# Strassen block products in the second matmul of an FFN: seven products of halves for seven of nine token blocks

## The chip, the cores and the metric

One Trainium2 chip, one core of it. The metric is the device time of one execution in microseconds (us), and the kernel before was timed in three runs: 1028.28, 1029.17 and 1034.58 us, median 1029.17 us. TensorE (PE) multiplies, with its weight loads (PEld) beside it; VectorE (DVE), ScalarE (ACT) and GpSimd (POOL) do the elementwise work; SyncE (SP) issues most of the transfers.

## What is computed

Attention over 4 batches of 576 tokens and 8 heads (block-causal, blocks of 64), then two layers with a feed-forward network (FFN) each. The change concerns the second one:

```
X = fft(fft(x, axis=1), axis=2)
u = x + real(X)
un = (u - mean(u)) / sqrt(var(u) + 1e-6)
ch = relu(un @ w_ch1) @ w_ch2          # 512 -> 2048 -> 512
out = u + ch
```

All of it is in float32 precision. The kernel reaches that with float16 matmuls: every operand is kept as a part `hi` (float16 of the value) and a part `lo` (float16 of what is left), and a product is three matmuls: hi*hi, hi*lo and lo*hi, summed in PSUM.

## The kernel before

The 2304 tokens stand in nine blocks of 256: E0 to E3 and F0 to F3 (first and folded second part of each batch) and L (what is left of all four). `X[c]` holds a block's tokens as two tiles of 128 rows, 512 float32 features wide.

For a block the second FFN runs in three steps. **LN** (`ln`, `ln_hi`, `ln_lo`, L442 to L501) norms the two tiles, splits them on ACT (L491) and DVE (L497) and has SP transpose them by DMA (L498) into `xnT`, of which there is one buffer: a block's transposes can start only when the first product of the block before has read it. **g1** (`gemm1`, L513) makes the 2048 hidden features in eight slots: a slot is 24 matmuls of 256 columns (L530) into one of five PSUM banks, and `g1_out` empties it with two instructions, ReLU into `hi` on ACT (L539) and `max(x,0) - hi` into `lo` on DVE (L540). **g2** (`gemm2`, L547; `gemm2_both` for E0, L577) multiplies by `w_ch2`: for each of the two token tiles 16 x 3 matmuls of 512 columns (L555, L585) into one bank, and `g2_out` (L564) adds the scaled result to `X` into an extra tile on DVE (L570) and SP writes it out (L575).

The second FFN's blocks go E0, F0, E1, F1, E2, F2, E3, F3, L. `ffn_items` writes them as g1 of a block, then its g2, with the LN steps of the next block between the last four parts of the g2. The DFT (`dft_*`) runs beside the first of these blocks and ends in `dft_b_left` (pool tile `u`, L1203 to L1216) while F0's g1 runs. Its constants and the first half of `w_ch1` (two tiles) live in one SBUF pool, `dpool`, which stays open to the end. Another pool has nine slots of 8 KB per partition, tag `w`; from here on they hold the second half of `w_ch1` (two) and all of `w_ch2` (four, until F0's g2 is over). `w_ch2` comes as int64 bits in float64, is decoded once, spilled to DRAM as float32, read back (L373) and split with its scales (L300, L308).

The order of the work is made twice. `merge` (L1022) takes the streams' items by a virtual clock (each item has a cost and things it needs) and calls them; then the framework sorts each engine's instructions by priority (`tc.high_priority(n)` moves them forward) into one fixed order per engine, in which each instruction waits for semaphores. Every engine works strictly in its order.

Of the kernel before, what the change touches and what calls it, by code (L numbers as in the profile page):

```python
# [82 lines left out]

@with_exitstack
def fused_kernel(ctx: ExitStack, tc: tile.TileContext, io: dict):
# [203 lines left out]
    def w_hi(ffn, which, c):  # L289
# [90 lines left out]
    def w_items():  # L380

# [181 lines left out]

    def g2_out(ffn, c, t, ps):  # L564
        x = X[c]
        if ffn == 1:
            dst = x[:, t, :]
        else:
            dst = D_["p"].tile([128, 2, DM], F32, tag=("xe", "xo")[t], name="out")[:, 0]
        nc.vector.scalar_tensor_tensor(  # L570
            out=dst, in0=ps, scalar=W["inv", ffn][:, 0:1], in1=x[:, t, :],
            op0=ALU.mult, op1=ALU.add,
        )
        if ffn == 2:
            nc.sync.dma_start(out=io["out"][slot_of[c] + t], in_=dst)  # L575
# [17 lines left out]
    def ffn_slots(ffn, c):
        s = []
        for mp in range(MT // 2):
            s.append((2.62, lambda mp=mp: gemm1(ffn, c, mp)))
        for t in range(2):
            for part in range(4):
                s.append((2.59, lambda t=t, part=part: gemm2(ffn, c, t, part)))
        return s  # L600
# [649 lines left out]
    if True:  # L1250
# [40 lines left out]
        def ffn_items(ffn, order, both=(), mixed=None):  # L1291
            seq = []
            for n, c in enumerate(order):
                x = ("X", ffn, c) if ffn == 2 else ("X1", c)
# [182 lines left out]
```

## Time and profile before

| | us |
|---|---|
| three runs | 1028.28, 1029.17 (median), 1034.58 |
| span of the profiled execution, first to last instruction | 1034.0 |
| PE busy | 941.8 (91%) |
| DVE busy | 618.7 (60%) |
| ACT busy | 501.4 (48%) |

The profiled execution's own time is not given apart from its span; among the three runs only the slowest, 1034.58 us, is as long as the span, so that is taken for it: span 1034.0 us and 0.6 us around it. In the page's slices a digit is the busy share of 1/40 of the span (25.85 us) in tenths, and in its row PEclk the clock that TensorE was granted. A matmul's duration in a group of lines includes its way through the array; the time from one to the next is read from the chain of waits, whose row gives the total of so many.

### The profile page before, as it was taken

What the parts mean: (1) busy time and instruction counts of PE and PEld (TensorE: products, weight loads), DVE (VectorE), ACT (ScalarE), POOL (GpSimd) and SP (SyncE); (2) the same over time, 40 slices, a digit from 0 to 9 for tenths busy, and PEclk for the clock granted to TensorE, in tenths of its full rate; (3) what the DMA queues carried; (4) which work ended last, traced back from release to release, by engine and by line L of the source; (5) the groups of instructions that cost most, each with busy time, mean ns of one, the idle gap of its engine ahead of it and who ended that gap; (6) DMA issues with size and microseconds to landing.
All of it is one profiled execution on the core that took longest, in us unless ns stands there. A gap on an engine that the chain in (4) does not pass through costs nothing.

```text
span 1034.0 us, 18330 instructions
## 1 busy us (share of the span) xinstructions
PE 941.8 (91%) x7226; PEld 642.5 (62%) x7226; DVE 618.7 (60%) x1501; ACT 501.4 (48%) x884; POOL 83.6 (8%) x217
## 2 busy tenths in 40 slices
PE   5476869898989989999998979999999999999998
PEld 3464744475575575676584746767668577586673
DVE  4799888686867876774396979864332332222120
ACT  5698965676767677534366665632111021120110
POOL 2100101001102002040011111100000000000000
PEclk8588989899999999999998989999999999999999
DMA  7995834666658668456315375620010100201100
GB/s 215 234 253 154 257 72 113 130 130 139 148 96 173 125 128 151 73 138 176 72 60 128 87 226 202 217 77 18 25 31 11 41 21 22 31 22 31 31 11 21
DMA packets 172439, 110.84 MB, mean 107 GB/s; under 512 B 146893, under 2 KB 155094, under 8 KB 170816
## 3 DMA queue, kind: packets, MB, share of 16 engines
q1 hardware_dynamic: 170032, 105.41, 41.3%
q0 software_dynamic: 2320, 4.25, 1.8%
q8 instruction: 57, 0.93, 0.4%
q14 instruction: 30, 0.25, 0.1%
HBM read 59.95 MB, written 11.01 MB: 69 GB/s over the span
## 4 chain that ended last, share of the span: by engine, by line
PE 44%; DVE 6%; DMA 5%; ACT 2%; issue 1%; POOL 0%; ACTq 0%; DVEq 0%; POOLq 0%
PE g L530 19%; PE g L555 19%; DMA wr<-in_w 4%; PE g L585 3%; DVE ws L215 1%; ACT wr L233 1%; DMA xnT1L<-xs 1%; DVE hT L540 1%; PE pq L1189 1%; ACT sign L208 1%; PE ya L1158 1%; DVE ws L212 1%; DVE wq L308 1%; PE pq L1179 1%; PE pf L1179 1%
## 5 line engine op out<-in xcount | busy, mean ns | idle before, releaser
L530 PEld LDWEIGHTS <-wq 128*128 128x128 f16 x3456 | 337.7, 99 | 69.0 <-ACT wq L300 8.2
L555 PE MATMUL g<-wq,hT 128*128 128x512 f16 x1440 | 334.8, 382 | 0.0
L555 PEld LDWEIGHTS <-hT 128*128 128x128 f16 x1440 | 140.7, 98 | 164.8 <-issue 9.6
L539 ACT ACTIVATE hT<-g 128x512 f16<-128x512 f32 x144 | 84.7, 591 | 244.0 <-PE g L530 243.9
L540 DVE SCALAR_TENSOR_TENSOR hT<-g,hT 128x512 f16<-128x512 f32 x144 | 98.6, 687 | 138.6 <-ACT hT L539 138.2
L679 PE MATMUL pv<-vh,PT 128*128 128x65 f16 (+1 forms) x800 | 105.2, 203 | 33.5 <-DMA PT<-P 30.5
L679 PEld LDWEIGHTS <-PT 128*128 128x128 f16 x1200 | 83.6, 100 | 57.7 <-DMA PT<-P 33.1
L891 PE MATMUL st<-k,qz 128*128 128x512 f16 (+2 forms) x288 | 81.5, 338 | 15.8 <-ACT e L913 15.8
L913 ACT ACTIVATE e<-st,aq,acf 128x384 f32<-128x384 f32 (+2 forms) x80 | 56.8, 741 | 60.9 <-DVE aq L908 54.8
L704 DVE SCALAR_TENSOR_TENSOR P<-e,P 128x768 f16<-128x768 f32 (+2 forms) x64 | 62.0, 971 | 38.2 <-ACT P L703 38.0
L585 PE MATMUL g<-wq,hT 128*128 128x512 f16 x288 | 66.6, 389 | 0.3 <-DVE wq L308 0.3
L679 PE MATMUL pv<-vl,PT 128*128 128x64 f16 (+1 forms) x400 | 65.8, 202 | 0.1
L703 ACT ACTIVATE P<-e 128x768 f16<-128x768 f32 (+2 forms) x64 | 54.7, 859 | 5.0 <-DMA PT<-P 3.6
L491 ACT ACTIVATE xs<-xn 128x512 f16<-128x512 f32 x36 | 22.4, 626 | 62.2 <-DMA xnT2('E', 3)_10327<-xs 7.9
L497 DVE TENSOR_TENSOR xs<-xn,xs 128x512 f16<-128x512 f32 x36 | 24.7, 687 | 46.0 <-ACT xs L491 46.0
L195 ACT ACTIVATE ws<-wr 128x512 f32<-128x512 f32 (+1 forms) x48 | 39.3, 829 | 26.2 <-DMA wr<-in_w 23.7
L907 DVE TENSOR_REDUCE aq<-st 128x2 f32<-128x768 f32 (+2 forms) x48 | 46.6, 973 | 8.7 <-PE st L891 5.1
L212 DVE SCALAR_TENSOR_TENSOR ws<-ws,sign 128x512 int32<-128x512 int32 (+1 forms) x48 | 41.5, 867 | 17.2 <-ACT sign L208 14.0
L208 ACT ACTIVATE sign<-wr 128x512 f16<-128x512 f32 (+1 forms) x48 | 46.7, 974 | 9.3 <-DMA wr<-in_w 4.8
L585 PEld LDWEIGHTS <-hT 128*128 128x128 f16 x288 | 28.7, 100 | 34.6 <-issue 3.1
L731 PE MATMUL st<-raw 128*128 128x128 f32 (+1 forms) x128 | 37.3, 421 | 12.2 <-ACT e L749 7.0
L215 DVE SCALAR_TENSOR_TENSOR ws<-wr,ws 128x512 int32<-128x512 int32 (+1 forms) x48 | 41.3, 862 | 0.4
(387 smaller groups left out, 1296.2 us busy)
## 6 DMA issues: line engine op xcount, KB each, us to landing
wr<-in_w SPq DMA_DIRECT2D x16, 1024.0 KB, 6.3
wr<-in_w SPq DMA_DIRECT2D x32, 512.0 KB, 4.1
rawv<-in_vt SPq DMA_DIRECT2D x16, 320.0 KB, 3.7
rawqk<-in_kt SPq DMA_DIRECT2D x16, 288.0 KB, 2.8
out<-out SPq DMA_DIRECT2D x18, 256.0 KB, 2.0
d<-ws SPq DMA_DIRECT2D x4, 1024.0 KB, 5.1
ws<-d SPq DMA_DIRECT2D x4, 1024.0 KB, 8.0
rawqk<-in_qt SPq DMA_DIRECT2D x32, 80.0 KB, 3.4
```

Source lines behind the costliest of these rows:

```text
L208: nc.scalar.activation(out=z[:, :, :, 1], in_=hw.bitcast(F32), func=AF.Copy, scale=float(2.0 ** -100))
L212: nc.vector.scalar_tensor_tensor(out=di, in0=di, scalar=3, in1=zi, op0=ALU.logical_shift_left, op1=ALU.bitwise_or)
L530: nc.tensor.matmul(out=ps[:, i, :], lhsT=w1(ffn, k, wh, m), rhs=xt[:, xh, k, :], start=(n == 0), stop=(n == 3 * KT - 1),)
L539: nc.scalar.activation(out=h[:, :, 0, :], in_=ps, func=AF.Relu)
L540: nc.vector.scalar_tensor_tensor(out=h[:, :, 1, :], in0=ps, scalar=0.0, in1=h[:, :, 0, :], op0=ALU.max, op1=ALU.subtract,)
L555: nc.tensor.matmul(out=ps, lhsT=h[f // 4][:, f % 4, hh, t * 128:(t + 1) * 128], rhs=w2(ffn, f, wh), start=(f == 0 and hh == 0 and wh == 0) ...
L585: nc.tensor.matmul(out=g2["b"][t], lhsT=h[f // 4][:, f % 4, hh, t * 128:(t + 1) * 128], rhs=w2(ffn, f, wh), start=(f == 0 and hh == 0 and ...
L679: nc.tensor.matmul(out=out[..., 0:w], lhsT=l, rhs=v[..., 0:w], start=(n == 0), stop=(n == len(mm) - 1))
L703: nc.scalar.activation(out=P[:, 0, 0:n], in_=e, func=AF.Copy, scale=PSC)
L704: nc.vector.scalar_tensor_tensor(out=P[:, 1, 0:n], in0=e, scalar=PSC, in1=P[:, 0, 0:n], op0=ALU.mult, op1=ALU.subtract)
L891: nc.tensor.matmul(out=st[:, h, 0:n] if j < 4 else sf[:, o:o + n], lhsT=qz[:, a, q:q + 128], rhs=k[:, c, o:o + n], start=(i == 0), stop=(j ...
L913: nc.scalar.activation(out=e[:, h], in_=st[:, h], func=AF.Exp, scale=cf, bias=nb[:, h:h + 1],)
```

## The change

Seven of the second FFN's blocks (all but E0 and F0) take another way through both products.

Second product (`s_gemm2_steps`): the block's hidden features are halved by feature (0 to 1023, 1024 to 2047) and by token tile, `w_ch2` is halved by feature and by output column, and in place of eight products of halves there are seven, of sums and differences of halves (Strassen's algorithm in Winograd's form). A product is 8 x 3 matmuls of 256 columns into one of three PSUM banks. The first two products (`mm(1)`, `mm(2)`) leave out their last eighth (i = 7) until both have done i = 0 to 6. `got(p)` adds a product, or a running sum `su`, to quarters of `X` in place; `put(t)` writes a tile out.

First product (`s_gemm1`): slot i makes features i and i + 8 (of 16 tiles of 128), so that both halves lie in the same bank, and `s_out` empties it in eight instructions where there were two: two ReLUs on ACT into a float32 tile `r`, four sums and differences of 128 columns on DVE, one copy of 896 columns on ACT (`hi` of seven operands), one subtraction of 896 columns on DVE (`lo`). They go into tiles `hs` of the tag `w`.

Weights (`t_items`): the DFT's pool is closed after `dft_b_left`, and a pool of seven tiles T (56 KB per partition) opens in its place; each T is one of the seven operands made of `w_ch2`'s halves. `w_ch2` is read back from DRAM a second time (`wt`, four loads of 1 MB, for j = 0 and j = 1 two each), and for each j and each T: for four of the seven a subtraction on DVE (1024 columns, chained), a copy on ACT (1024 columns, `hi`) and a multiply and subtract on DVE (1024 columns, `lo`). `t_balance` works out power-of-two scales, some eleven instructions on at most four columns. The `w_ch1` tiles of `dpool` get a pool of their own, and outputs of all blocks of the second FFN are now made in place in `X`.

```
 def w_tile(ffn, which, c):
     if ffn == 2 and which == 1:
-        return wst["pool"].tile([128, 2, 2048], F16, tag="w", bufs=2, name=f"wq{ffn}{which}{c}")
+        return wst["w1"].tile([128, 2, 2048], F16, tag="w", bufs=2, name=f"wq{ffn}{which}{c}")
...
+    def t_items(close, needs):
...
+        def build(j, nm):
+            a, b = src[j, 0], src[j, 1]
...
+            x, y, z = {
+                "B11": (b11, None, None), "B21": (b21, None, None), "B22": (b22, None, None),
+                "T1": (b11, b12, b11), "T3": (b12, b22, b12), "T2": (b11, b22, b11),
+                "T4": (b21, b21, b11),
+            }[nm]
+            if y is not None:
+                nc.vector.tensor_tensor(out=x, in0=y, in1=z, op=ALU.subtract)
+            sc = W["tk"][:, 4 + j:5 + j]
+            f = slice(4 * j, 4 * j + 4)
+            nc.scalar.activation(out=T[nm][:, 0, f], in_=x, func=AF.Copy, scale=sc)
+            nc.vector.scalar_tensor_tensor(
+                out=T[nm][:, 1, f], in0=x, scalar=sc, in1=T[nm][:, 0, f],
+                op0=ALU.mult, op1=ALU.subtract,
+            )
...
 def g2_out(ffn, c, t, ps):
     x = X[c]
-    if ffn == 1:
-        dst = x[:, t, :]
-    else:
-        dst = D_["p"].tile([128, 2, DM], F32, tag=("xe", "xo")[t], name="out")[:, 0]
+    dst = x[:, t, :]
...
+    def s_out(ps, h, j):
+        r = fpool.tile([128, 8, 128], F32, tag="hT", bufs=4, name="hr")
+        rf = r.rearrange("p b t -> p (b t)")
+        for q in range(2):
+            nc.scalar.activation(
+                out=rf[:, 256 * q:256 * q + 256], in_=ps[:, q, :], func=AF.Relu,
+                scale=W["tk"][:, j + 2 * q:j + 2 * q + 1],
+            )
+        for o, a, b, op in (
+            (4, 0, 2, ALU.add), (6, 1, 0, ALU.subtract), (5, 4, 1, ALU.subtract),
+            (7, 3, 5, ALU.subtract),
+        ):
+            nc.vector.tensor_tensor(out=r[:, o], in0=r[:, a], in1=r[:, b], op=op)
+        nc.scalar.activation(out=h[:, 0], in_=r[:, 1:8], func=AF.Copy)
+        nc.vector.tensor_tensor(out=h[:, 1], in0=r[:, 1:8], in1=h[:, 0], op=ALU.subtract)
...
+        def mm(p, hb, nm, i0=0, i1=8):
+            if i0 == 0:
+                st[p] = d_tile("s2")
+            ps = st[p][:, 0:256]
+            for i in range(i0, i1):
+                h = hT[2, c][i // 2][:, i % 2]
+                for hh, wh in ((0, 0), (0, 1), (1, 0)):
+                    nc.tensor.matmul(
+                        out=ps, lhsT=h[:, hh, hb], rhs=T[nm][:, wh, i],
+                        start=(i == 0 and hh == 0 and wh == 0), stop=(i == 7 and hh == 1),
+                    )
...
+        return [
+            (2.3, lambda: mm(1, A11, "B11", 0, 7)),
+            (2.3, lambda: mm(2, A12, "B21", 0, 7)),
+            (0.6, lambda: (
+                mm(1, A11, "B11", 7, 8), got(1), mm(2, A12, "B21", 7, 8), got(2),
+            )),
+            (2.6, lambda: (mm(6, S2, "T2"), got(6))),
+            (2.6, lambda: (mm(5, S1, "T1"), got(5))),
+            (2.6, lambda: (mm(7, S3, "T3"), got(7))),
+            (2.6, lambda: (mm(3, S4, "B22"), got(3), put(1))),
+            (2.6, lambda: (mm(4, A22, "T4"), got(4), put(0))),
+        ]
...
+                if ffn == 2 and c not in PLAIN2:
+                    g1 = [(2.62, lambda i=i, c=c: s_gemm1(c, i), (("W", 2, 1, 3),), None) for i in range(8)]
...
+        WT = t_items(dctx.close, (("X", 2, "L"), ("W", 2, 2, 3)))
...
+            (S_D, R_T, WT),
```

PE's order is unchanged up to the end of F0's g2. Three places after that show what is new. The first is DVE in the g1 of block F1; before, one instruction per slot (`g1` is the bank, `hT` the hidden features):

```order
L540 SCALAR_TENSOR_TENSOR hT_9311<-g1_9312,hT_9311 128x2x256
L540 SCALAR_TENSOR_TENSOR hT_9311<-g1_9339,hT_9311 128x2x256
L540 SCALAR_TENSOR_TENSOR hT_9366<-g1_9367,hT_9366 128x2x256
L540 SCALAR_TENSOR_TENSOR hT_9366<-g1_9394,hT_9366 128x2x256
L540 SCALAR_TENSOR_TENSOR hT_9421<-g1_9422,hT_9421 128x2x256
```

and now (`hr` is the tile r of a slot, `hs` its seven operands):

```order
L701 TENSOR_TENSOR hr_9616<-hr_9616 128x128 x4
L703 TENSOR_TENSOR hs2_9590<-hr_9616,hs2_9590 128x896
L701 TENSOR_TENSOR hr_9650<-hr_9650 128x128 x4
L703 TENSOR_TENSOR hs2_9590<-hr_9650,hs2_9590 128x896
L701 TENSOR_TENSOR hr_9685<-hr_9685 128x128 x4
```

A slot's four sums stand behind the `lo` (L703) of the slot before, and that `lo` behind ACT's copy (L702) of its own slot; ACT's order is two ReLUs and the copy, slot by slot.

The second place is DVE behind the end of the DFT (`u` is its last result) in F0's g1; before, four slots are emptied and the LN of E1 and F1 follows:

```order
L1216 TENSOR_TENSOR XxL_3227<-XxL_3227,u_8704 128x512
L540 SCALAR_TENSOR_TENSOR hT_8709<-g1_8710,hT_8709 128x2x256
L540 SCALAR_TENSOR_TENSOR hT_8709<-g1_8737,hT_8709 128x2x256
L540 SCALAR_TENSOR_TENSOR hT_8764<-g1_8765,hT_8764 128x2x256
L540 SCALAR_TENSOR_TENSOR hT_8764<-g1_8792,hT_8764 128x2x256
```

and now the 22 instructions of the T tiles stand among them; the end of that stretch, the last of which stands ahead of everything of E1's g1 (`wt11` is the last load, `g2_8940` the second half of F0's g2):

```order
L440 TENSOR_TENSOR wt10_8867<-wt11_8869,wt10_8867 128x4x256
L444 SCALAR_TENSOR_TENSOR tB21_8757<-wt11_8869,tk_8135,tB21_8757 128x1024
L444 SCALAR_TENSOR_TENSOR tB22_8758<-wt11_8869,tk_8135,tB22_8758 128x1024
L444 SCALAR_TENSOR_TENSOR tT3_8760<-wt10_8867,tk_8135,tT3_8760 128x1024
L440 TENSOR_TENSOR wt10_8867<-wt11_8869,wt10_8867 128x4x256
L577 TENSOR_TENSOR xs_9457<-xn_9455,xs_9457 128x512
L440 TENSOR_TENSOR wt11_8869<-wt11_8869,wt10_8867 128x4x256
L444 SCALAR_TENSOR_TENSOR tT2_8761<-wt10_8867,tk_8135,tT2_8761 128x1024
L647 SCALAR_TENSOR_TENSOR XxF0_3226<-g2_8940,winv2_8146,XxF0_3226 128x512
L444 SCALAR_TENSOR_TENSOR tT4_8762<-wt11_8869,tk_8135,tT4_8762 128x1024
```

So T's last four tiles for j = 1 wait for the fourth load, and the last one also for F0's result. The third place is SP's queue, where that load stands (`xnT2` are the transposes):

```order
L427 DMA wt00_8763<-d220_7394 128x2048
L427 DMA wt01_8765<-d222_7877 128x2048
L427 DMA wt10_8867<-d221_7657 128x2048
L652 DMA out_0<-XxE0_204 128x512 x2
L578 DMA_TRANSPOSE xnT2('E', 1)_8972<-xs_8987 128x8x128
L427 DMA wt11_8869<-d223_8044 128x2048
L578 DMA_TRANSPOSE xnT2('E', 1)_8972<-xs_9005 128x8x128
```

Three loads find free slots of the tag `w` early. `wt11` takes the slot of `wt00`, so it waits until DVE has used that for the last time (T2 of j = 0), and E1's second transpose is queued behind it.

## Rows read from the trace of the kernel before

**Rows 1.** The page's 40 slices: busy tenths and granted clock.
```profile
PE   5476869898989989999998979999999999999998
DVE  4799888686867876774396979864332332222120
PEclk8588989899999999999998989999999999999999
```
**Rows 2.** Chain of waits, its end: start us, us, engine, what, line, count.
```profile
666.14 20.72 PE g L585 x96
...
738.43 20.96 PE g L530 x192
759.39 20.72 PE g L555 x96
...
1009.47 20.73 PE g L555 x96
1030.23 0.75 DVE out L570
```
**Rows 3.** Timeline of ACT and DVE: two slots of E1's g1, then three dependent DVE instructions.
```profile
741.09 0.60 ACT L539 ACTIVATE hT<-g 128x512 f16<-128x512 f32 x1 [13.94 <-PE g L530]
741.71 0.69 DVE L540 SCALAR_TENSOR_TENSOR hT<-g,hT 128x512 f16<-128x512 f32 x1 [2.50 <-ACT hT L539]
...
704.06 0.47 DVE L1207 SCALAR_TENSOR_TENSOR u<-pq,dinv,qc 128x256 f32<-128x256 f32 x1
704.57 0.69 DVE L1213 TENSOR_TENSOR XxE<-XxE,u 128x512 f32<-128x512 f32 x1
705.18 0.69 DVE L1216 TENSOR_TENSOR XxF<-XxF,u 128x512 f32<-128x512 f32 x1
```
**Rows 4.** Groups by line and shape, whole span: count, busy us, mean ns, idle before.
```profile
L958 DVE TENSOR_TENSOR N<-pv,rr 128x128 f32<-128x128 f32 x32 | 9.2, 287 | 0.4
L497 DVE TENSOR_TENSOR xs<-xn,xs 128x512 f16<-128x512 f32 x36 | 24.7, 687 | 46.0 <-ACT xs L491 46.0
L1118 DVE TENSOR_TENSOR xo<-XxE,XxF 128x1024 f32<-128x1024 f32 x4 | 4.9, 1218 | 0.0
L1075 DVE SCALAR_TENSOR_TENSOR ge<-xe,dsc,ge 128x1024 f16<-128x1024 f32 x4 | 5.1, 1276 | 0.2 <-ACT ge L1074 0.2
L703 ACT ACTIVATE P<-e 128x768 f16<-128x768 f32 x32 | 27.2, 849 | 1.8 <-DMA PT<-P 1.4
L703 ACT ACTIVATE P<-e 128x1024 f16<-128x1024 f32 x16 | 16.9, 1057 | 1.6 <-DMA PT<-P 0.9
L1199 ACT ACTIVATE qc<-pq,dinv 128x255 f32<-128x255 f32 x8 | 3.8, 473 | 8.3 <-PE pq L1189 8.2
```
**Rows 5.** Timeline of DVE: end of the DFT, then the LN statistics of F2.
```profile
709.35 0.69 DVE L1216 TENSOR_TENSOR XxL<-XxL,u 128x512 f32<-128x512 f32 x1
...
728.49 0.18 DVE L449 BATCH_NORM_AGGREGATE ln2('F', 2)_9952<-bn2('F', 2)0_9953 128x2 f32<-128x6 f32 x1
...
732.48 0.16 DVE L466 SCALAR_TENSOR_TENSOR ln2('F', 2)_9952<-ln2('F', 2)_9952 128x2 f32<-128x2 f32 x1
```
**Rows 6.** DMA issues from 660 us on, with KB and us to landing.
```profile
ws<-d SPq DMA_DIRECT2D x2, 1024.0 KB, 7.6
xnT2('E', 1)_8903<-xs SPq DMA_TRANSPOSE x2, 3.6
```
**Rows 7.** Stretches: us, then busy PE, PEld, DVE, ACT, POOL, granted clock, DMA share, GB/s.
```profile
297.40:299.80 2.40, 0.00 (x0) 0.00 (x0) 2.40 (x6) 1.60 (x3) 0.00 (x0) 1.00 0.57 158
299.80:301.80 2.00, 1.93 (x10) 1.43 (x11) 2.00 (x6) 0.00 (x0) 0.00 (x0) 0.54 0.95 225
...
421.10:422.70 1.60, 0.11 (x2) 0.04 (x1) 0.54 (x3) 1.54 (x3) 0.00 (x0) 1.00 0.00 0
423.00:425.00 2.00, 2.00 (x19) 1.29 (x18) 0.70 (x1) 1.84 (x3) 0.00 (x0) 1.00 0.00 0
...
617.00:619.00 2.00, 2.00 (x8) 0.95 (x7) 2.00 (x6) 0.52 (x1) 0.00 (x0) 0.50 0.89 301
```

More of the change, by code (lines that the diff above doesn't have):

```diff
@@ L274, in w_balance, with t_balance @@
         W["inv", ffn] = inv
+    def t_balance():
+        s1, s2 = W["sc", 2, 1], W["sc", 2, 2]
+        z = sm.tile([128, 8], F32, tag="tz", bufs=1, name="tz")
+        eta, m2, r1 = z[:, 0:2], z[:, 2:4], z[:, 4:8]
+        nc.vector.tensor_tensor(out=eta, in0=s1[:, 0:2], in1=s1[:, 2:4], op=ALU.min)
+        nc.vector.tensor_scalar(out=eta, in0=eta, scalar1=0.5, scalar2=None, op0=ALU.mult)
+        nc.vector.tensor_tensor(out=m2, in0=s2[:, 0:2], in1=s2[:, 2:4], op=ALU.min)
+        nc.vector.scalar_tensor_tensor(
+            out=m2, in0=m2, scalar=0.5, in1=eta, op0=ALU.mult, op1=ALU.mult
+        )
+        zeta = sm.tile([128, 1], F32, tag="tzeta", bufs=1, name="tzeta")
+        nc.vector.tensor_reduce(out=zeta, in_=m2, axis=AX.X, op=ALU.min)
+        k = W["tk"] = cpool.tile([128, 7], F32, name="tk")
+        nc.vector.reciprocal(out=k[:, 6:7], in_=zeta)
+        nc.vector.reciprocal(out=r1, in_=s1)
+        for h in range(2):
+            nc.vector.tensor_tensor(
+                out=k[:, 2 * h:2 * h + 2], in0=eta, in1=r1[:, 2 * h:2 * h + 2], op=ALU.mult
+            )
+        nc.vector.reciprocal(out=m2, in_=eta)
+        nc.vector.tensor_scalar(
+            out=k[:, 4:6], in0=m2, scalar1=zeta[:, 0:1], scalar2=None, op0=ALU.mult
+        )
     def w_jobs(ffn, which, c):
@@ L370, in w_back2 @@
         if c == 0:
+            t_balance()
             w_balance(2)
@@ L378, in w_end2, with t_open, load @@
         w_lo(2, 2, c)
+    T = {}
+    def t_open(close):
+        close()
+        tp = ctx.enter_context(tc.tile_pool(name="tpool", bufs=1))
+        for nm in BLOCKS:
+            T[nm] = tp.tile([128, 2, 8, 256], F16, name="t" + nm)
+    def t_items(close, needs):
+        src = {}
+        def load(j):
+            for h in range(2):
+                t = wpool.tile([128, 4, 512], F32, tag="w", bufs=9, name=f"wt{j}{h}")
+                nc.sync.dma_start(out=t.rearrange("p i f -> p (i f)"), in_=W["dram", 2, 2, j + 2 * h])
+                src[j, h] = t
+        def build(j, nm):
+            a, b = src[j, 0], src[j, 1]
+            b11, b12 = a[:, :, 0:256], a[:, :, 256:512]
+            b21, b22 = b[:, :, 0:256], b[:, :, 256:512]
+            x, y, z = {
[8 more added lines that the diff above has]
+            nc.scalar.activation(out=T[nm][:, 0, f], in_=x, func=AF.Copy, scale=sc)
+            nc.vector.scalar_tensor_tensor(
+                out=T[nm][:, 1, f], in0=x, scalar=sc, in1=T[nm][:, 0, f],
+                op0=ALU.mult, op1=ALU.subtract,
+            )
+        out = [(0.0, lambda: t_open(close), needs, None), (0.0, lambda: load(0), (), None)]
+        for j in range(2):
+            for nm in BLOCKS:
+                out.append((
+                    1.0, lambda j=j, nm=nm: build(j, nm), (),
+                    ("W", 2, "T") if (j, nm) == (1, BLOCKS[-1]) else None,
+                ))
+            if j == 0:
+                out.append((0.0, lambda: load(1), (), None))
+        return out
     def w_items():
@@ L591, in gemm2_both, with s_gemm1 @@
                 g2_out(ffn, c, t, g2["b"][t])
[L593 to L600, printed above, removed]
+    def s_gemm1(c, i):
+        if i % 2 == 0:
+            t = wpool.tile([128, 2, 2, 7, 128], F16, tag="w", bufs=9, name=f"hs{i}")
+            hT[2, c] = hT.get((2, c), []) + [t]
+        xt = xnT[2, c]
+        ps = g_tile([128, 2, 256], "g1")
+        for q in range(2):
+            n = 0
+            for k in range(KT):
+                for wh, xh in ((0, 0), (0, 1), (1, 0)):
+                    nc.tensor.matmul(
+                        out=ps[:, q, :], lhsT=w1(2, k, wh, i + 8 * q), rhs=xt[:, xh, k, :],
+                        start=(n == 0), stop=(n == 3 * KT - 1),
+                    )
+                    n += 1
+        prio(s_out, S7P)(ps, hT[2, c][i // 2][:, i % 2], i // 4)
@@ new lines, in s_gemm2_steps, with x_add, u_add, got @@
+    def s_gemm2_steps(c):
+        st = {}
+        x = X[c]
+        inv = W["tk"][:, 6:7]
+        def mm(p, hb, nm, i0=0, i1=8):
[5 more added lines that the diff above has]
+                for hh, wh in ((0, 0), (0, 1), (1, 0)):
+                    nc.tensor.matmul(
+                        out=ps, lhsT=h[:, hh, hb], rhs=T[nm][:, wh, i],
+                        start=(i == 0 and hh == 0 and wh == 0), stop=(i == 7 and hh == 1),
+                    )
+        def x_add(t, d, p=None):
+            o = x[:, t, 256 * d:256 * d + 256]
+            nc.vector.scalar_tensor_tensor(
+                out=o, in0=st["u"] if p is None else st[p][:, 0:256], scalar=inv, in1=o,
+                op0=ALU.mult, op1=ALU.add,
+            )
+        def u_add(p):
+            nc.vector.tensor_tensor(out=st["u"], in0=st["u"], in1=st[p][:, 0:256], op=ALU.add)
+        @(lambda f: prio(f, YP))
+        def got(p):
+            if p == 1:
+                st["u"] = wpool.tile([128, 256], F32, tag="w", bufs=9, name="su")
+                nc.scalar.activation(out=st["u"], in_=st[1][:, 0:256], func=AF.Copy)
+                x_add(1, 0, 1)
+            elif p == 2:
+                x_add(1, 0, 2)
+            elif p == 6:
+                u_add(6)
+                x_add(0, 0)
+            elif p == 5:
+                u_add(5)
+                x_add(1, 1)
+                x_add(0, 1)
+            elif p == 7:
+                x_add(0, 1, 7)
+                x_add(0, 0, 7)
+            elif p == 3:
+                x_add(1, 1, 3)
+            else:
+                x_add(0, 0, 4)
+        def put(t):
+            nc.sync.dma_start(out=io["out"][slot_of[c] + t], in_=x[:, t, :])
+        A11, A22, A12, S1, S2, S3, S4 = range(7)
+        return [
[10 more added lines that the diff above has]
+        ]
```

21 lines of the change are left out of this document (19 added, 2 removed).

## The prediction

> **What bounds the kernel now.** I read the slices first. From the 27th slice on (about 670 us) PE is at 9 in every slice and its clock at 9, while DVE falls from 7 to 2 [rows 1]. The chain of waits says the same more sharply: from F0's second product to the end it consists of PE alone, and DVE adds 0.75 us behind the last matmul [rows 2]. So in the part that the change touches, the time is PE's count of columns, and every wait that the change gives PE is paid in full. The chain also gives the pace: 192 matmuls of 256 columns in 20.96 us, 109.2 ns each; 96 of 512 columns in 20.72 us [rows 2]. A g1 slot of 24 matmuls is 24 x 109.2 ns = 2.62 us. DVE and ACT have room only as a sum; what counts is whether the eight instructions of a slot can follow each other within 2.62 us. For that I read the timeline for what lies between dependent instructions [rows 3], and the groups for durations [rows 4].
>
> The sum is made against the profiled execution: span 1034.0 us, about 1034.6 with what lies around it, 5.4 above the median of 1029.17. A difference found here is put on that median. A measurement of this kernel can tell about 1% from no change, 10.3 us: below 1018.9 is faster, above 1039.5 slower.
>
> **What is removed.** A changed block's second product has 7 x 24 = 168 matmuls of 256 columns in place of 96 of 512: 168 x 109.2 ns = 18.34 us against 20.72 [rows 2], -2.38 us. Seven blocks: **-16.6 us**. The first product keeps its matmuls.
>
> **The slot's chain, in six blocks (F1, E2, F2, E3, F3, L).** An ACT instruction starts 0.04 us after PE's end; between ACT's end and DVE's start lie 0.02 us (741.09 + 0.60 to 741.71); an independent DVE instruction starts 0.08 us ahead of the end of the one before it (704.57 + 0.69 = 705.26 against 705.18), a dependent one 0.04 us behind it (704.06 + 0.47 to 704.57) [rows 3]. A sum of 128 columns takes 287 ns [rows 4]. The four start at 0, 0.21, 0.42 (its operand is two back) and 0.75 us (it needs the third) and end at 1.04. ACT's copy of 896 columns lies midway between 768 (849 ns) and 1024 (1057 ns): 0.95 us. The `lo` of 896 lies between 687 ns for 512 columns and 1218 for 1024 [rows 4]: 0.687 + 384/512 x 0.531 = 1.08 us. DVE's order is sums(i), lo(i), sums(i + 1), and lo(i) waits for ACT's copy of sums(i); so the three lie in a ring: 1.04 + 0.03 + 0.95 + 0.03 + 1.08 - 0.08 = **3.05 us per slot**, against PE's 2.62. The two ReLUs of the next slot run on ACT under the `lo` and cost nothing there.
>
> In the first slot the ReLUs take 0.04 + 0.39 + 0.47 = 0.90 us (473 ns for 255 columns [rows 4]), the chain after them 1.04 + 0.03 + 0.95 + 0.03 + 1.08 = 3.13. The last slot's `lo` therefore ends 0.90 + 7 x 3.05 + 3.13 = 25.4 us behind the end of slot 0, which is 25.4 - 18.34 = 7.06 us after the first product's end; slot 6's `lo` at +4.01 and its `hi` at +2.9.
>
> What PE has to do until then: `mm(1)` and `mm(2)` without i = 7 are 42 matmuls, 4.59 us. But i = 6 needs slot 6. From the end of g1: i = 0 to 5, 18 matmuls, to 1.97; wait for `hi` to 2.9, two matmuls; wait for `lo` to 4.01, the third, to about 4.14; 21 matmuls of the second product to 6.43, two more with the last `hi` to 6.65; wait for the last `lo` to about 7.08; four matmuls, 0.44, to 7.52. Without waits these 48 matmuls are 5.24 us. The wait is 2.28 us per block, six blocks: **+13.7 us**. Bounds for the term: 0, if the ring takes 2.62 us or less (the last slot alone then needs 0.9 + 3.13 = 4.03 us, under the 4.6 that are covered), and 3.7 per block (22 us), if each of the ring's hops costs 0.15 us in place of 0.03. I take the middle value, since all three of its durations have a near row.
>
> **E1: the T tiles.** They are built on DVE: 14 multiply-subtracts of 1024 columns at 1.28 us and 8 subtractions at 1.22 [rows 4], 27.7 us in all. PE's work of that time, F0's second product, is not touched. DVE begins behind the DFT's last add, 709.35 + 0.69 = 710.04 [rows 5], and ACT's first copy (1.06 + 0.07), so at 711.2. The first half (7 + 4 instructions, 13.8 us) with the hidden `lo`s of F0 between reaches T2 at about 726.5. Only then can the fourth load go out; it takes 7.6 us to land [rows 6], to 734.1. DVE has 2.5 us of nothing there. Behind it stand 5 multiply-subtracts and 3 subtractions, 10.1 us, and about 1.3 us of LN and F0's result: T ends at about 745.2, whereas E1's first slot is ready at 738.43 + 2.62 = 741.05 [rows 2]. E1's chain starts 4 us late, has the LN statistics of the next blocks between its slots (in the kernel before 728.49 to 732.64 [rows 5]; I put 2 us), and its last `lo` comes at 745.2 + 8 x 3.05 + 2 = 771.6, slot 6's at 768.6. PE ends the first product at 759.39 [rows 2] and then gets three matmuls per 3.05 us.
>
> What such a trickle does to the clock: after the pause at 609 to 615 the engine was at 0.50, and still at 0.50 while it was busy 2.00 of 2.00 us [rows 7]. So I take half clock for the 21 matmuls of the second product (4.6 us) from 768.7 and recovery at the end: all 48 are done at about 773.7, not 764.6 (759.39 + 5.24): **+9 us**. At full clock it is 771.6 + 0.5, so +7.5. Bounds: 4, if the T tiles end before E1's first slot, and 12, if LN costs its whole 4 us. E1's second transpose is queued on SP behind the fourth load, which goes out at 726.5; with 3.6 us to land [rows 6] it is there at about 730, and 8 us of F0's second product are left as cover, so E1's g1 starts where it did.
>
> **The small parts.** The last instruction is an add of 256 columns, 0.47 us by the like form in rows 3, in place of 512, 0.75 us [rows 2]: **-0.3**. `t_balance`, eleven instructions of 0.16 to 0.18 us like the LN's [rows 5], stands ahead of the split of `w_ch2`: 0, covered by PE's work in E0, 2 us if not. The reordered rows between 570 and 690 us on ACT, DVE and SP: 0, within 2 either way; PE's order there is the same. Results in place in `X`: 0; nobody reads `X` after them. The adds of `got` wait for their own product only, and three banks leave each 2.6 us of cover.
>
> **The sum.** -16.6 + 13.7 + 9 - 0.3 = **+5.8 us**: 1034.6 + 5.8 = 1040.4 against the profiled execution, and 1029.2 + 5.8 = **1035.0** on the median. What the seven products save is given back at the seams between the two products.
>
> **Rivals.**
> *The emptying keeps pace* (ring at or below 2.62 us, so no wait in six blocks; E1's last `lo` at 745.2 + 8 x 2.62 + 2 = 768.2, about +5 with the clock): -16.6 + 5 - 0.3 = -12, **1017.2 us**. For it: the ring is only 0.43 us too long, and an ACT copy to float16 or a `lo` of a quicker kind would close it. Against it: all its parts have rows within 15% of their width.
>
> *The clock falls at every seam*; this ends on the slower side. Each seam has two pauses of 0.9 us, parted by two matmuls, and a third of 0.4. For it: after a pause of 2.40 us at 297.4 the next stretch ran at 0.54 with PE busy 1.93 of 2.00 us; against it: after one of 1.60 us at 421.1 the clock stayed at 1.00 [rows 7]. The sum of a seam's pauses, 2.3, lies near the first. It decides from the point where a seam costs the clock: then the 21 matmuls behind it and some more run at half for about 3.5 us, +1.7 per block, six blocks +10: **1045 us**.
> The Trainium skill ("TensorE: Matmul & The Clock Gate", section "HAM oscillation — how this bites in real kernels") says that bursts of matmuls parted by waits for data can fall to half rate at each burst, which speaks for this rival; the two pauses of this trace agree with it once and once not.
>
> *The T tiles come much later.* The sources are quarters of a tile, cut in four pieces. If that makes the operations of 1024 columns 1.5 times as long, T2 comes at 733.4, the fourth load at 741.0, the last T at 757.5 and E1's last `lo` at 757.5 + 8 x 3.05 + 2 = 783.9: E1 +20 in place of +9, the sum +16.8: **1046 us**. For it: no row shows an operand in pieces of 256 columns. Against it: the width alone set the durations in the groups read, 1218 and 1276 ns for 1024 columns [rows 4].
>
> **How the numbers follow.** The forecast gets 0.50; its own range is 1029 to 1040. The emptying keeps pace 0.28, the clock 0.15, late T tiles 0.07. Faster by over 1%: 0.23 of the first rival's 0.28, for a part of it ends between 1019 and 1022. Slower: 0.04 of the forecast, 0.12 of the clock's case, all of the third: 0.23. Within 1%: 0.46 + 0.05 + 0.03 = 0.54. The range from 1014 to 1047 holds the forecast, most of the first rival and most of the other two.
>
> **What would show it.** Right: in the trace after, g1 of F1 begins each `lo` about 3.05 us behind the last; PE has idle time at the first product's end in every changed block, ended by DVE's `lo`, 2 to 2.5 us, and 7 to 9 at E1; between the seams 168 matmuls in 18.3 us. Wrong: a `lo` period of 2.62 us (then the ring is overrated), a clock under 0.9 in the slices behind 800 us (the second rival), E1's g1 starting after 739 (the third), or time lost ahead of 700 us, where I count none.

## The result, and the profile after

The changed kernel took 1037.0 us (median of four runs, 1035.1 to 1038.49) against 1029.13 us of the kernel before (1028.28 to 1034.58): a ratio of 1.0069, 95% interval 1.0042 to 1.0096. It is slower by less than 1%. The forecast was 1035.0 and "within 1%".

The profiled execution of the changed kernel has a span of 1036.6 us. Its slices answer to [rows 1]: behind E1's seam (the 8 in slice 30) PE stays at 9 up to the last slice, in the last twelve slices DVE is at 3 to 8 where it was at 0 to 3, and the clock's digits stay at 9.

```profile
PE   5576879998889989999998989999989999999997
DVE  5799898676867776675488988959856565464543
PEclk9688989999999999999998989999999999999999
```

The chain of waits answers to [rows 2] (start us, us, engine, what, line, count). Before, it was PE alone from F0's second product on. Now it leaves PE in every changed block, goes through `hr`, `hs` (ACT) and `hs` (DVE), and comes back to PE in the second product:

```profile
774.73 2.63 PE g L681 x24
...
800.15 18.00 PE s L719 x148
818.15 2.63 PE g L681 x24
846.66 13.71 PE s L719 x124
860.38 2.63 PE g L681 x24
...
989.43 2.63 PE g L681 x24
1014.84 18.01 PE s L719 x148
```

A row of 24 `g` matmuls is the first slot of a block, so the distances between those rows are whole blocks: F1 43.42 us (774.73 to 818.15), E2 42.23 (818.15 to 860.38), then by further rows F2 43.41, E3 42.22, F3 43.42, and L 43.42 to its last matmul (1014.84 + 18.01). Without a wait a block is 20.96 + 18.34 = 39.30 us; before it was 20.96 + 20.72 = 41.68 [rows 2]. So four seams cost 4.12 us and two (E2, E3) 2.93: 22.3 us in six blocks.

The timeline of PE shows the seams of E1, F1 and E2 (in brackets the idle time ahead of a row, and what ended it):

```profile
728.78 21.12 PE L681 MATMUL g<-xnT2('E', 1)_8972,wq 128*128 128x256 f16 x192
749.74 1.80 PE L719 MATMUL s<-tB,hs 128*128 128x256 f16 x15
...
757.00 4.42 PE L719 MATMUL s<-tB,hs 128*128 128x256 f16 x26 [0.73 <-DVE hs L703]
...
774.57 21.12 PE L681 MATMUL g<-xnT2('F', 1)_9427,wq 128*128 128x256 f16 x192
...
799.02 0.39 PE L719 MATMUL s<-tB,hs 128*128 128x256 f16 x2 [1.37 <-ACT hs L702]
800.15 4.90 PE L719 MATMUL s<-tB,hs 128*128 128x256 f16 x28 [0.73 <-DVE hs L703]
...
842.44 0.39 PE L719 MATMUL s<-tB,hs 128*128 128x256 f16 x2 [1.37 <-ACT hs L702]
843.57 2.79 PE L719 MATMUL s<-tB,hs 128*128 128x256 f16 x24 [0.73 <-DVE hs L703]
846.66 0.61 PE L719 MATMUL s<-tB,hs 128*128 128x256 f16 x4 [0.30 <-DVE hs L703]
```

E1's second product takes 774.57 - 749.74 = 24.83 us. E2's seam is the one that the prediction described: a wait for the `hi` of slot 6, two matmuls, a wait for its `lo`, 21 matmuls of the second product, and a wait for slot 7. In F1 the pauses are the same, but the rows behind them run longer (28 matmuls in 4.90 us, where E2 has 24 in 2.79). The stretches of PE's clock tell why (us, then busy PE, PEld, DVE, ACT, POOL, granted clock, DMA share, GB/s):

```profile
801.00:803.00 2.00, 2.00 (x11) 1.45 (x10) 0.93 (x2) 1.47 (x2) 0.00 (x0) 0.50 0.04 8
...
844.00:846.00 2.00, 2.00 (x21) 1.79 (x20) 0.89 (x3) 1.47 (x2) 0.00 (x0) 1.00 0.00 0
```

In F1 the granted clock goes to 0.50 (of its two levels the lower one, 1.2 GHz) behind the pauses; in E2 it stays at 1.00. E1, F2, F3 and L have such a stretch too, E3 has none.

DVE's timeline shows the T tiles ahead of E1, and the ring in F1's g1:

```profile
701.82 1.29 DVE L444 SCALAR_TENSOR_TENSOR tB<-wt,tk,tB 128x1024 f16<-128x1024 f32 x1 [1.27 <-ACT tB L443]
...
722.37 1.22 DVE L440 TENSOR_TENSOR wt<-wt,wt 128x1024 f32<-128x1024 f32 x1
...
731.83 1.27 DVE L444 SCALAR_TENSOR_TENSOR tT<-wt,tk,tT 128x1024 f16<-128x1024 f32 x1
...
...
786.60 1.09 DVE L703 TENSOR_TENSOR hs<-hr,hs 128x896 f16<-128x896 f32 x1 [1.07 <-ACT hs L702]
787.61 1.01 DVE L701 TENSOR_TENSOR hr<-hr 128x128 f32<-128x128 f32 x4
789.70 1.09 DVE L703 TENSOR_TENSOR hs<-hr,hs 128x896 f16<-128x896 f32 x1 [1.07 <-ACT hs L702]
```

From one `lo` (L703) to the next it is 789.70 - 786.60 = 3.10 us. In each period DVE works 2.02 us and stands still for 1.07, waiting for ACT's copy of the slot whose sums it has just made.

The two profiles differ by only 2.6 us in span, but from E1's g1 to the end the changed kernel takes 1036.6 - 728.78 = 307.8 us, and the kernel before 1034.0 - 738.26 = 295.7 (E1's g1 in the same view; 738.43 in the chain of [rows 2]): 12 us more. The rest, 9.5 us, lies ahead of E1, where the prediction counted nothing; the first experiment is on that.

### The profile page after: what moved, and what is told of

Same layout as the page of the kernel before. It is cut to its first block, busy times and chain, and to the rows that moved or that the text cites. A ratio compares the mean times of both kernels' runs of the same rounds, so it can differ in the third digit from the quotient of the medians.

```text
span 1036.6 us, 19852 instructions
## 1 busy us (share of the span) xinstructions
PE 930.3 (90%) x7730; PEld 692.9 (67%) x7730; DVE 739.8 (71%) x1821; ACT 578.6 (56%) x1017; POOL 82.8 (8%) x217
## 4 chain that ended last, share of the span: by engine, by line
PE 28%; DVE 20%; ACT 7%; DMA 2%; issue 2%; POOL 0%; ACTq 0%; DVEq 0%; POOLq 0%
PE s L719 11%; PE g L610 6%; DVE hs L703 5%; ACT hs L702 5%; PE g L635 5%; DVE hr L701 5%; PE g L662 2%; DMA wr<-in_w 2%; PE g L681 2%; DVE tT L444 1%; DVE hT L620 1%; DVE wt L440 1%; DVE ws L220 1%; DVE ws L217 1%; ACT wr L238 1%
## 5 line engine op out<-in xcount | busy, mean ns | idle before, releaser
L635 PE MATMUL g<-wq,hT 128*128 128x512 f16 x768 | 185.9, 381 | 0.0
L719 PEld LDWEIGHTS <-hs 128*128 128x128 f16 x1176 | 117.8, 101 | 39.4 <-ACT hs L702 13.2
L635 PEld LDWEIGHTS <-hT 128*128 128x128 f16 x768 | 74.4, 98 | 85.1 <-issue 7.1
L703 DVE TENSOR_TENSOR hs<-hr,hs 128x896 f16<-128x896 f32 x56 | 61.1, 1092 | 57.8 <-ACT hs L702 57.8
L702 ACT ACTIVATE hs<-hr 128x896 f16<-128x896 f32 x56 | 53.2, 950 | 80.1 <-DVE hr L701 74.9
L693 ACT ACTIVATE hr<-g,tk 128x256 f32<-128x256 f32 x112 | 46.1, 462 | 80.9 <-PE g L681 80.9
L719 PE MATMUL s<-tB,hs 128*128 128x256 f16 x504 | 68.6, 296 | 17.6 <-ACT hs L702 11.1
L719 PE MATMUL s<-tT,hs 128*128 128x256 f16 x672 | 75.8, 273 | 0.0
L620 DVE SCALAR_TENSOR_TENSOR hT<-g,hT 128x512 f16<-128x512 f32 x88 | 59.8, 683 | 18.3 <-ACT hT L619 18.1
L701 DVE TENSOR_TENSOR hr<-hr 128x128 f32<-128x128 f32 x224 | 56.6, 287 | 18.6 <-ACT hr L693 15.8
L662 PE MATMUL g<-wq,hT 128*128 128x512 f16 x288 | 65.5, 385 | 0.3 <-DVE wq L338 0.3
```

Source lines behind the costliest of these rows:

```text
L620: nc.vector.scalar_tensor_tensor(out=h[:, :, 1, :], in0=ps, scalar=0.0, in1=h[:, :, 0, :], op0=ALU.max, op1=ALU.subtract,)
L635: nc.tensor.matmul(out=ps, lhsT=h[f // 4][:, f % 4, hh, t * 128:(t + 1) * 128], rhs=w2(ffn, f, wh), start=(f == 0 and hh == 0 and wh == 0) ...
L662: nc.tensor.matmul(out=g2["b"][t], lhsT=h[f // 4][:, f % 4, hh, t * 128:(t + 1) * 128], rhs=w2(ffn, f, wh), start=(f == 0 and hh == 0 and ...
L701: nc.vector.tensor_tensor(out=r[:, o], in0=r[:, a], in1=r[:, b], op=op)
L702: nc.scalar.activation(out=h[:, 0], in_=r[:, 1:8], func=AF.Copy)
L703: nc.vector.tensor_tensor(out=h[:, 1], in0=r[:, 1:8], in1=h[:, 0], op=ALU.subtract)
```

## The experiments

**e1, the kernel before again.** No edit.

> The kernel before once more, for a second profile. In the two profiles at hand E1's g1 begins at 738.43 us before and at 728.78 after, 9.65 us earlier, though I counted nothing ahead of that point. Theory 'chance of that profile': 7.4 of the 9.65 us had gathered by 557 us, where both kernels have the same order, so another profile of the kernel before begins E1's g1 at 730 to 733 us and has a span of 1026 to 1028. Rival 'the early part became quicker': it begins at 737 to 739 again, with a span of about 1033.

Its second profile has a span of 1026.4 us, and E1's g1 begins 7.6 us earlier than in the first (timeline of PE):

```profile
730.63 21.12 PE L530 MATMUL g<-xnT2('E', 1)_8903,wq 128*128 128x256 f16 x192
```

From there to the end it is 295.8 us, as in the first profile. So the first profile was a slow one in its early part, and the change didn't quicken that part by 10 us. In the eight profiles of the changed kernel and its variants, E1's g1 begins between 728.8 and 733.4 us, around the 730.6 here. The 12 us behind E1 are the change.

**e5, the changed kernel again.** No edit, beside e6 and e7.

> The changed kernel once more, beside the next two on the same chip. From E1's g1 to the end it should again take about 307.8 us against 295.8 of the kernel before (12 us more: six seams, E1's wait, less the saved columns). If the early part is the same in both kernels, as the second profile of the kernel before says (E1's g1 at 730.6 there), E1's g1 begins at 729 to 733 us.

1041.35 us (1037.62 to 1043.4) against 1030.79 (1026.28 to 1035.69) of the kernel before on this chip; ratio 1.0086, 1.0052 to 1.012. E1's g1 begins at 728.97 us and the span is 1036.7: 307.7 us again. Two things differ. E1's second product takes 25.90 us (749.93 to 775.83) in place of 24.83. And the seams with the fallen clock are partly other ones: E1, E2, E3 and L here. In the chain of waits F1's seam is now a short one (124 matmuls from its last wait to the next block) and E2's a long one:

```profile
804.52 13.71 PE s L719 x124
...
843.65 18.00 PE s L719 x148
```

**e2, copy and `lo` split.** The first three operands come straight from the ReLUs, so their copy needs no sum:

```
+        nc.scalar.activation(out=h[:, 0, 0:3], in_=r[:, 1:4], func=AF.Copy)
         for o, a, b, op in (
...
-        nc.scalar.activation(out=h[:, 0], in_=r[:, 1:8], func=AF.Copy)
-        nc.vector.tensor_tensor(out=h[:, 1], in0=r[:, 1:8], in1=h[:, 0], op=ALU.subtract)
+        nc.scalar.activation(out=h[:, 0, 3:7], in_=r[:, 4:8], func=AF.Copy)
+        nc.vector.tensor_tensor(out=h[:, 1, 0:3], in0=r[:, 1:4], in1=h[:, 0, 0:3], op=ALU.subtract)
+        nc.vector.tensor_tensor(out=h[:, 1, 3:7], in0=r[:, 4:8], in1=h[:, 0, 3:7], op=ALU.subtract)
```

> ACT's copy and DVE's lo of a slot are split in two, 384 columns that come straight from the ReLUs and 512 that need the sums; the first copy runs beside the sums. Theory 'ring' (sums, copy and lo in a row take 3.10 us per slot against PE's 2.62, and the lag ends at the seam between the products): the row becomes sums 1.04, lo of 384 0.55, lo of 512 0.69 with the copy beside them, about 2.4 us, so the lo period falls to PE's 2.62 us, the six seams lose their waits (4.1 and 2.9 us now) and E1 keeps 1 to 2 of 6.65: about -27 us against the changed kernel, 1008 to 1014 us. Rival 'the seam itself' (PE loses time there by its clock or by the change of operands, whatever DVE does): the period falls as well but 2 to 4 us per seam stay, 1025 us or more.

1012.77 us (1009.48 to 1015.76) against 1030.82 (1026.96 to 1034.92); ratio 0.9819, 0.9791 to 0.9848. This is faster than both kernels. DVE still waits for ACT, but less, and has something to do in between:

```profile
827.62 0.69 DVE L705 TENSOR_TENSOR hs<-hr,hs 128x512 f16<-128x512 f32 x1 [0.70 <-ACT hs L703]
828.23 0.81 DVE L702 TENSOR_TENSOR hr<-hr 128x128 f32<-128x128 f32 x3
828.96 0.55 DVE L704 TENSOR_TENSOR hs<-hr,hs 128x384 f16<-128x384 f32 x1
829.43 0.28 DVE L702 TENSOR_TENSOR hr<-hr 128x128 f32<-128x128 f32 x1
830.41 0.69 DVE L705 TENSOR_TENSOR hs<-hr,hs 128x512 f16<-128x512 f32 x1 [0.70 <-ACT hs L703]
```

The period is 830.41 - 827.62 = 2.79 us, not PE's 2.62 as expected: the last sum stands behind the first `lo`, so that `lo` stayed in the ring ahead of the second copy. But the lag is then small enough for the 4.6 us of cover. PE's timeline of E2 has no wait at all, and the second product takes 852.85 - 834.50 = 18.35 us:

```profile
834.50 5.40 PE L721 MATMUL s<-tB,hs 128*128 128x256 f16 x48
...
852.85 2.35 PE L681 MATMUL g<-xnT2('F', 2)_10471,wq 128*128 128x256 f16 x20
```

All six seams are like this (18.33 to 18.35 us, L 18.49), E1 keeps 19.88 - 18.34 = 1.5 us, and no half clock is seen behind E1's start. "The seam itself" falls: where no operand is late, a seam costs nothing.

**e6, the copy alone split.** The first `+` line of above and the second copy; the `lo` stays one instruction of 896 columns behind everything.

```
+        nc.scalar.activation(out=h[:, 0, 0:3], in_=r[:, 1:4], func=AF.Copy)
...
-        nc.scalar.activation(out=h[:, 0], in_=r[:, 1:8], func=AF.Copy)
+        nc.scalar.activation(out=h[:, 0, 3:7], in_=r[:, 4:8], func=AF.Copy)
```

> Only ACT's copy is split (384 columns beside the sums, 512 behind them); DVE's work and its order stay exactly as they are. Theory 'ring': the row sums, copy, lo falls by what the copy loses, 0.95 to 0.62 us (the group of 512 columns), so the lo period is 3.10 - 0.33 = 2.77 us; the last lo comes 0.90 + 1.04 + 0.06 + 0.62 + 1.09 + 7 x (2.77 - 2.62) = 4.8 us behind the first product's end, where PE needs it at 4.6: about 0.2 us per seam, E1's wait about 3.5: -24 us, 1011 to 1015 us. Rival 'DVE has too much work per slot' (its instructions, not the waiting between them, fill the period): DVE's work is unchanged, so the period stays 3.10 and the time within 2 us of the changed kernel's.

1019.09 us (1017.14 to 1021.29) against 1030.79; ratio 0.9868, 0.9841 to 0.9895. That is 22 us less than the changed kernel beside it (e5), where 24 were expected. In DVE's timeline, and below it PE's of E2:

```profile
834.20 1.09 DVE L704 TENSOR_TENSOR hs<-hr,hs 128x896 f16<-128x896 f32 x1 [0.69 <-ACT hs L703]
835.21 1.14 DVE L702 TENSOR_TENSOR hr<-hr 128x128 f32<-128x128 f32 x4
837.04 1.09 DVE L704 TENSOR_TENSOR hs<-hr,hs 128x896 f16<-128x896 f32 x1 [0.70 <-ACT hs L703]
...
835.61 2.35 PE L720 MATMUL s<-tB,hs 128*128 128x256 f16 x20
838.19 3.45 PE L720 MATMUL s<-tB,hs 128*128 128x256 f16 x28 [0.24 <-DVE hs L704]
...
854.58 21.12 PE L681 MATMUL g<-xnT2('F', 2)_10447,wq 128*128 128x256 f16 x192
```

The period fell to 2.84 us (837.04 - 834.20) with every DVE instruction as it was; expected was 2.77, and the four sums take 1.14 us here where they took 1.01. PE waits 0.24 us for E2's slot 6, and a second product takes 18.97 us (854.58 - 835.61) in place of 18.34, 0.6 more where 0.2 was expected. So it is the wait for ACT inside the ring that made the period, not the amount of DVE's work. That amount rose in the split of both, which is faster still.

**e3, three products ahead of the last slots.** PE works on i = 0 to 5 of products 1, 2 and 6 before it needs slot 6:

```
-            (2.3, lambda: mm(1, A11, "B11", 0, 7)),
-            (2.3, lambda: mm(2, A12, "B21", 0, 7)),
-            (0.6, lambda: (
-                mm(1, A11, "B11", 7, 8), got(1), mm(2, A12, "B21", 7, 8), got(2),
-            )),
-            (2.6, lambda: (mm(6, S2, "T2"), got(6))),
+            (1.97, lambda: mm(1, A11, "B11", 0, 6)),
+            (1.97, lambda: mm(2, A12, "B21", 0, 6)),
+            (1.97, lambda: mm(6, S2, "T2", 0, 6)),
+            (1.96, lambda: (
+                mm(1, A11, "B11", 6, 7), mm(2, A12, "B21", 6, 7), mm(6, S2, "T2", 6, 7),
+                mm(1, A11, "B11", 7, 8), got(1), mm(2, A12, "B21", 7, 8), got(2),
+                mm(6, S2, "T2", 7, 8), got(6),
+            )),
```

> The emptying stays as it is; PE does i = 0 to 5 of three products (1, 2 and 6) first, then i = 6 of the three, then i = 7. Theory 'ring': the lo period stays 3.10 us and the last lo still comes about 7.4 us behind the first product's end, but PE now has 6.9 us of work until then in place of 4.6; so the six seams shrink from 4.1 and 2.9 us to about 0.5 with no fall of the clock, and E1's from 6.65 to about 3.4: -20 to -22 us, 1015 to 1017 us. Rival 'the seam itself': the waits on hs may go, but 2 us or more per seam stay, 1025 us or more.

1046.75 us (1045.47 to 1049.93) against 1030.82; ratio 1.0154, 1.0131 to 1.0177: slower than the changed kernel, where 20 us less was expected; by the number alone this is the rival's side. PE's timeline of E2:

```profile
848.81 0.61 PE L719 MATMUL s<-tB,hs 128*128 128x256 f16 x4 [0.48 <-DVE hs L703]
...
852.47 1.68 PE L681 MATMUL g<-xnT2('F', 2)_10423,wq 128*128 128x256 f16 x7 [2.72 <-DMA xnT2('F', 2)_10423<-xs]
854.33 6.05 PE L719 MATMUL s<-tT,hs 128*128 128x256 f16 x48 [0.19 <-DVE XxE L726]
```

The seam itself did what the ring says: 0.48 us of wait for `hs`, as forecast. What I had not counted is the three banks. Now all three finish together and the next product needs one of them emptied; and in the order that the framework made, matmuls of F2's first product stand ahead of it, which wait for F2's transpose. In DVE's timeline the adds that empty the bank stand behind an LN step that waits for ACT, which waits for that same transpose:

```profile
853.19 0.69 DVE L577 TENSOR_TENSOR xs<-xn,xs 128x512 f16<-128x512 f32 x1 [3.26 <-ACT xs L571]
853.80 0.48 DVE L726 SCALAR_TENSOR_TENSOR XxE<-s,tk,XxE 128x256 f32<-128x256 f32 x1
```

So 2.4 us of waiting for operands (1.37 + 0.73 + 0.30 above) became 2.7 us of waiting for a transpose, with the bank free no sooner than that. And the clock, which was expected to stay up, falls behind this pause in five of the seven seams (F1, E2, F2, E3, F3). In E2 the stretch behind the pause is at 0.50, and the 7 matmuls of 1.68 us above run in it:

```profile
852.47:854.33 1.86, 1.68 (x7) 1.03 (x8) 1.14 (x3) 0.90 (x2) 0.00 (x0) 0.50 0.00 0
```

The wait for `hs` at E2's seam shrank as the ring says, so the run doesn't speak against it; but what rules the rival out is e2, not this run. It shows that here, with all three banks in use, the cover cost more than it saved.

**e4, E1 plain.** `PLAIN2` gets `("E", 1)`; E1 keeps the old two products.

> E1 keeps the old two products too, so six blocks are changed. Theory 'T tiles': E1's 6.65 us of waiting beyond its 18.34 us come from the T tiles on DVE ahead of its first slot; plain it takes 20.96 + 20.72 us, so -6.65 + 2.38 = -4.3 us, about 1032.7, and F1's seam stays at 4.1 us. Rival 'E1 is a seam like the others' (ring and clock alone, about 4.1 us of the 6.65): the T tiles then cost elsewhere, F1's seam grows by 2 us or more, and the time stays within 2 us of 1037.

1035.76 us (1032.23 to 1038.26) against 1030.82; ratio 1.0038, 1.0015 to 1.006. The interval of the time leaves both theories standing, the trace doesn't:

```profile
753.42 20.88 PE L635 MATMUL g<-wq,hT 128*128 128x512 f16 x96
774.14 2.13 PE L681 MATMUL g<-xnT2('F', 1)_9326,wq 128*128 128x256 f16 x18
...
816.39 0.82 PE L681 MATMUL g<-xnT2('E', 2)_9781,wq 128*128 128x256 f16 x6
```

E1's second product takes 20.72 us (753.42 to 774.14) in place of 24.83, and F1's 21.29 (795.10 to 816.39), no more than an ordinary seam: the T tiles cost nothing where a plain block covers them. The theory as I wrote it is still too simple, because in E1 an ordinary seam goes too.

**e8, T tiles without their `lo`.** The 14 multiply-subtracts are left out, GpSimd writes zeros; the outputs lack that part of the second product.

```
-            nc.vector.scalar_tensor_tensor(
-                out=T[nm][:, 1, f], in0=x, scalar=sc, in1=T[nm][:, 0, f],
-                op0=ALU.mult, op1=ALU.subtract,
-            )
+            nc.gpsimd.memset(T[nm][:, 1, f], 0.0)
```

> The changed kernel without the 14 multiply-subtracts that make the lo half of the T tiles (17.9 us of DVE; GpSimd writes zeros there instead), so the outputs lack that part of the second product. Theory 'two parts of E1': E1's seam is the ordinary one of 2.9 to 4.1 us, and the 2.5 to 4.5 us beyond it come from the T tiles ahead of its first slot on DVE; so E1's second product takes 21.3 to 22.5 us, as in the other blocks, not 24.8 to 25.9. Rival 'E1 is longer for another reason' (the LN statistics between its slots, or its transposes): it stays at 24 us or more, or E1's g1 begins late.

One run, 1036.55 us; what counts is E1's seam in the trace. E1's second product takes 773.87 - 751.41 = 22.46 us, as F1's did in the changed kernel (22.45), with the same two pauses:

```profile
751.41 2.13 PE L716 MATMUL s<-tB,hs 128*128 128x256 f16 x18
754.91 0.39 PE L716 MATMUL s<-tB,hs 128*128 128x256 f16 x2 [1.38 <-ACT hs L699]
...
773.87 21.12 PE L678 MATMUL g<-xnT2('F', 1)_9427,wq 128*128 128x256 f16 x192
```

So E1's 6.5 us (24.83 - 18.34) are an ordinary seam of 4.1 and 2.4 us of T tiles; by e5's 25.90 us the T tiles' part is 3.4.

**e7, PE kept busy at the seam.** Ten idle matmuls ahead of i = 6 of the first product and six ahead of its third matmul; they write into the second product's bank, which that product then starts anew.

```
-            (2.3, lambda: mm(1, A11, "B11", 0, 7)),
+            (2.3, lambda: (mm(1, A11, "B11", 0, 6), fill(10), mm(1, A11, "B11", 6, 7, 6))),
```

> The changed kernel with idle matmuls (their result is overwritten) where PE waits at i = 6 of the first product: ten ahead of it, six ahead of its third matmul, so PE stands still for less. Nothing else moves; the lo period stays 3.10. Theory 'clock': in five of the seven seams the profile shows 3.4 us at half clock and those second products are 1.2 us longer (22.45 against 21.27); with PE kept busy the clock stays up and all are near 21.3 to 21.6: -5 to -6 us, about 1031. Rival 'no cost by the clock' (the waits absorb it: the matmuls at half clock only fill time in which lo is late anyway): the second products stay at 22.4 in those blocks even where no half clock is seen, and the time stays within 1.5 us.

1035.53 us (1033.63 to 1038.26) against 1030.79; ratio 1.0045, 1.0026 to 1.0063, beside 1.0086 of the changed kernel on that chip: 5.8 us between the medians, as expected, though the two intervals overlap a little. In E2 (L717 are the idle matmuls):

```profile
841.93 1.25 PE L717 MATMUL s<-tB,hs 128*128 128x256 f16 x10
843.47 0.39 PE L730 MATMUL s<-tB,hs 128*128 128x256 f16 x2 [0.29 <-ACT hs L702]
843.70 0.82 PE L717 MATMUL s<-tB,hs 128*128 128x256 f16 x6
```

No half clock is seen from E1 on, and the second products of F1 to F3 all take 21.27 to 21.29 us. From E1's g1 to the end it is 1034.1 - 731.32 = 302.8 us, 4.9 less than in the changed kernel beside it. The emptying was not touched (E1 alone got a new wait, 0.40 us for a bank), so the fallen clock cost about 1.2 us (22.45 - 21.28) in each ordinary seam where it fell.

## Why the prediction was right

**What is removed.** -2.38 us per block stands: without waits a second product took 18.34 us (e2).

**The ring.** Right in kind and nearly in size: 3.10 us per slot where 3.05 was worked out, and its parts as priced (copy 950 ns, `lo` 1092, a sum 287). e6 shows that it is the order and not the load: with DVE's work unchanged the period fell with ACT's copy. In a seam at full clock the wait was 2.93 us, not 2.28: over seven slots the small excess of the period adds up to some 0.5 us (F1's first is 3.22), and PE's waits follow the last `lo`. The upper bound of this term was added up wrongly: two hops 0.12 us longer in each of eight slots are 1.9 us more, 4.2 per block and not 3.7.

**The clock.** Here the forecast and its second rival both held in part. The term "13.7 us for six seams" was too small by 8.6: 6 x 0.65 = 3.9 us by the ring, and 4 x 1.19 = 4.8 by the clock, which I had put at nothing in the forecast and at 1.7 us per seam in the rival. It fell in four of the six, and by e7 at a lower price than the rival's, for part of what PE loses at half clock it would have waited anyway: E2 still waits 0.30 us for slot 7, F1 no longer does. The sign that was named for this rival, a clock under 0.9 in the slices, could not show it: 3.4 us at half clock take 0.07 off a slice of 25.9 us.
The Trainium skill ("TensorE: Matmul & The Clock Gate", section "HAM oscillation — how this bites in real kernels") describes bursts of matmuls parted by waits of about 3 to 5 us for data, each burst starting at half rate. The pauses here are shorter; the trace agrees with it in F1, F2, F3 and L, where the clock fell, and not in E2 and E3, whose pauses are the same.

**E1.** +9 was forecast, 6.5 came (7.6 in e5), of which 2.4 (3.4) by the T tiles (e8). The step that was too long is the idle time of DVE for the fourth load. In SP's timeline the load goes out when T2 is done, as predicted, and E1's second transpose behind it:

```profile
717.24 0.33 SPq L427 DMA_DIRECT2D wt<-d  x1
720.17 1.23 SPq L578 DMA_TRANSPOSE xnT2('E', 1)_8972<-xs  x1
```

It landed 4.9 us later, not 7.6 [rows 6], and until then DVE had the remaining work of the first three loads. So it never stood still there (its timeline has no wait between 701.82 and 733.10), and the T tiles ended 4.3 us behind the start of E1's g1 and not 6.8. E1's g1 was not held up.

**The early part.** Nothing was counted, and the second profile of before and those of the variants scatter around the same start of E1. The first profile, on which the sum was made, was slow there by 7.6 us. This doesn't matter to the sum, which was put on the median as a difference.

**The sum.** -16.7 + 22.3 + 6.5 = +12.1 us by the traces from E1 on, against +5.8 forecast: twice as much. The medians differ by only 7.9 us in the result and 10.6 beside e5. What makes up the other 1.5 to 4 us ahead of E1 isn't shown; the start of E1's g1 scatters by 4.6 us among the eight profiles, so it may be chance. That 1037.0 lies so near 1035.0 is therefore partly luck. The direction and the finding hold, that the saved columns are given back at the seams; the seams cost more than forecast, E1 less. The first rival (the emptying keeps pace, 1017.2 us) was wrong for this kernel, but it is nearly what e6 and e2 made of it: 1019.09 and 1012.77 us.

## What to carry to other kernels

When a bound engine gets fewer instructions but its operands more steps, don't add up the busy time of the helpers: write the steps of one slot down in the order of each engine and look for a ring, an engine that waits for another's answer to what it has just sent. Here DVE was idle for a third of each period and still the bound; cutting the copy so that a part of it runs beside the sums turned +0.9% into -1.3% (e5, e6), and with the `lo` cut as well it was -1.8% (e2). And before work is moved forward to cover a wait, count the buffers that it will hold until then.

## What the runs showed of the hardware

Two pauses of 1.37 and 0.73 us with two matmuls in between brought the clock from 1.00 to 0.50 in some seams and not in others of the same program, and in a second execution of it the seams had partly changed places (E1 and L in both, F1, F2 and F3 only in the first, E2 and E3 only in the second; in an ordinary seam it cost 1.2 us each time). With the pauses filled with idle matmuls, until those left in the six ordinary seams were about 0.3 us long, the clock stayed at 1.00 throughout (e7). It did so in E1 of that execution too, where pauses of 1.24, 0.73 and 0.60 us were left, so longer pauses don't bring it down each time. I had expected a pause of that length either to bring the clock down each time or never.
